# A fused attention and feed-forward kernel: all four-unit groups by 15 products per three feature blocks, and the scaling of r moved within the step for odd units

## The chip, the core and the metric

One core of one Trainium2 chip runs the whole kernel. The metric is the device time in microseconds (us) of one execution; the time of a kernel is the median of several runs.

## What is computed

Two blocks follow each other. The first is a linear attention with a decaying state; the second is a feed-forward block with a gate (SwiGLU), all in float32.

```python
for t in range(S):                     # r, k, v: (4, 8, 768, 48)
    cur = einsum(u * k[t], v[t])
    y[t] = einsum(r[t], state + cur)
    state = w * state + einsum(k[t], v[t])
x = y.transpose(0, 2, 1, 3).reshape(3072, 384)
g = x @ w_gate                         # (384, 1536)
out = (g * sigmoid(g) * (x @ w_val)) @ w_out     # w_out (1536, 384)
```

## The kernel before

**Units and groups.** The 3072 tokens are cut into 24 *units* of 128 tokens (`N`), in the order of time for all four batches at once. Attention turns unit i into a slice of `xT` (128 features x 3 x 128 tokens). Two units make a *group* g of 256 tokens for the feed-forward block, and from group 2 on the groups are worked in pairs g, g+1 (g even): such a pair, 512 tokens, is a *four-unit group*. The 1536 hidden features are 12 *feature blocks* f of 128.

**The feed-forward block.** Gate and value of a feature block are six 128x128 by 256-token matmuls per group if done directly. Groups 0 and 1 do that (`gate_value`, L451). The four-unit groups use forms with fewer products, in three kinds before the change:

- Groups 2 and 4: `four_units` (L648) with `four` (L599). Per feature block it makes 11 matmuls of 256 columns (L627), of sums of x (`x_sums`, L575: 4 VectorE additions per four-unit group) and sums of weights (`w_sums`, L585: 5 GpSimd additions of 128x256 per two feature blocks). Between the matmuls ScalarE copies partial results out of PSUM (L634), VectorE adds and multiplies (L637 to L645), ScalarE applies Silu (L607), and GpSimd makes one of the two products of gate and value (L611).
- Group 6: `three_beside` (L832) with `three_step` (L807). Per *three* feature blocks, called a round t of four, it makes 15 products, each of two matmuls of 256 columns (L817), one for the gate and one for the value. These are 120 matmuls per four-unit group. Each product is accumulated in one of the chains n, y, l4, l5, l1, l2, l8, each in a PSUM bank; ScalarE copies and VectorE additions of 128x512 (L842) take the chain's partial sums between the products, and the next product of a chain waits until its last sum is read. Silu is at L849. In rounds 0 to 2 GpSimd makes one gate-value product (z + 11.8) and VectorE two; value rows (`NR + 3 * j + i`) are written again in the next round.
- Groups 8 and 10: `three_units` (L927), the same products after the last unit, in the tail.

The 15-product forms need sums of x (`x_forms`, L761: 11 VectorE operations of 128x256), sums of weights (`w_forms`, L729: 9 GpSimd operations of 128x256 per round), and six of the weight blocks of every round replaced, once for good, by sums (`in_place`, L717: 6 GpSimd operations per round, 24 in all). `in_place` may run only after the last product with the plain weights. Before, 18 of the 24 run inside `four_units(4)` and the last 6 beside the projections that follow (`prepare_threes`, L791).

Each four-unit group ends in `two_projections` (L671): 14 products of 6 matmuls of 192 columns (L530), in the order of a list, with sums of the hidden values (`h_sums`, L495: 8 VectorE additions of 128x768) ahead of them. Tiles for sums of weights and for `h_sums` share one ring of three buffers (tag `w_bits`), so a new tile waits until the tile three before it is read. The first three pieces of the next group's products stand among the last four projections.

**Attention, by steps.** The loop over s (L1138) is written out by hand and sets the order on every engine. A step s from 12 on does in turn:

1. `own_sum(s)`; `scale(s+1)`: GpSimd scales k (L308) and r (L311) of unit s+1 from `k_ld`, `r_ld` into `hats`; `own_product(s+1)`: two more GpSimd operations (L235, L236); `load_v(s+1)` and `load(s+3)` on SyncE's queue.
2. `gaps(s, 0)`: pieces of the feed-forward work from `todo`. Then `scores(s-1)` (L382), `outputs(s-2)`, `update(s-2)`, and `gaps(s, 1)`.
3. `turn_blocks(s)` (L376): two VectorE transposes (L380) out of `blocks`. `move_blocks(s+1)` (L356): 16 small DMAs on SyncE's queue that bring `hats` of unit s+1 into `blocks`.
4. `gaps(s, 2)`, `diagonal(s)`, `gaps(s, 3)`, `gaps(s, 4)`.

From unit 12 on, units 2m and 2m+1 share one buffer for the scaled r (`rhat_of`, L110). So `scale_r` of an odd unit waits until the 16 DMAs of the even unit have read it. `gaps` hands out so many pieces per step that a four-unit group with its projections fills four steps; both `four_units` and `three_beside` give 26 pieces.

Of the kernel before, what the change touches and what calls it, by code (L numbers as in the profile page):

```python
# [9 lines left out]
FP32 = mybir.dt.float32  # L10
# [5 lines left out]
P = 128  # L16
# [6 lines left out]
def fast(  # L23
# [31 lines left out]
    N = B * NCH  # L55
# [29 lines left out]
    hTs = hv[:, 0:NR].rearrange("p (j f) t -> p j f t", j=2)  # L85
    sgs = cst.tile([P, 3, 2 * P], FP32, name="sgs")
    free_sg = deque(sgs[:, n] for n in range(3))
    free_part = deque(hv[:, NR + n] for n in range(6))

    banks = [ps_f.tile([P, 4 * P], FP32, name=f"bank{n}") for n in range(4)]  # L90
    free = deque(banks[:2])
# [1 line left out]
    def take():  # L93
        return free.popleft()
# [144 lines left out]
    def own_sum(i):  # L239
        dus[i] = three.tile([P, H], FP32, name="du", tag="du")  # L240
        dve.tensor_reduce(dus[i][:], rks.pop(i), axis=AX.X, op=ALU.add)
# [65 lines left out]
    def scale_k(i):  # L307
        pool.tensor_mul(khat[i % 4][:, :, 0:D], raw(i)[0], kscale)  # L308
# [11 lines left out]
    def scale(i):  # L320
        scale_k(i)
        scale_r(i)
# [187 lines left out]
    def project(g, n):  # L510
# [51 lines left out]

    PLACE = {
        "p1": 0, "p2": 3, "p6": 4, "c11": 5, "sg0": 6.5, "p7": 8, "p5": 9, "c22": 10, "p4": 12,
        "c21": 13, "p3": 17, "c12": 18, "sg1": 19.5, "h1": 24.5,
    }

    def x_halves(g):  # L570

        i = [2 * (g + j) % NX for j in range(2)]
        return [[xT[:, i[j] : i[j] + 2, c, :] for j in range(2)] for c in range(CC)]

    def x_sums(g):  # L575
        (x11, x12), (x21, x22), _ = x_halves(g)
        ta, tb = (two.tile([P, 2, 2, P], FP32, name=n, tag="w_low") for n in ("t12", "t34"))
        t1, t2, t3, t4 = ta[:, 0], ta[:, 1], tb[:, 0], tb[:, 1]
        dve.tensor_sub(t1, x12, x11)
        dve.tensor_sub(t2, x22, t1)  # L580
        dve.tensor_sub(t3, x22, x12)
        dve.tensor_sub(t4, x21, t2)
        part_of.setdefault(g, {})["t"] = (t1, t2, t3, t4)

    def w_sums(g, f):  # L585

        (w11, w12, w13), (w21, w22, w23) = (
            [w[:, c, P * f : P * (f + 2)] for c in range(CC)] for w in (wg, wv)
        )
        t = three.tile([P, 5, 2 * P], FP32, name="s", tag="w_bits")  # L590
        x = part_of.setdefault(g, {})
        x["s", f] = x["s", f + 1] = t
        pool.tensor_add(t[:, 0], w21, w22)
        pool.tensor_sub(t[:, 1], t[:, 0], w11)
        pool.tensor_sub(t[:, 2], w22, t[:, 1])
        pool.tensor_sub(t[:, 3], w12, t[:, 1])
        pool.tensor_sub(t[:, 4], w13, w23)

    def four(g, f, what):  # L599

        x = part_of[g]
        if what in ("p1", "p2"):
            x["ab"[what == "p2"], f] = take()
        h = [hT[g + j][:, f, :] for j in range(2)]
        if what in ("sg0", "sg1"):
            j = int(what[2])
            act.activation(h[j], h[j], AF.Silu)  # L607
            return
        if what == "h1":
            free_part.append(x.pop(("u3", f)))  # L610
            pool.tensor_mul(h[1], h[1], free_part[-1])  # L611
            return
        (w11, w12, w13), (_, w22, w23) = (
            [w[:, c, P * f : P * (f + 1)] for c in range(CC)] for w in (wg, wv)
        )
        (x11, _), (x21, x22), (x31, x32) = x_halves(g)
        s1, s2, s3, s4, s5 = (x["s", f][:, n, P * (f % 2) : P * (f % 2 + 1)] for n in range(5))
        t1, t2, t3, t4 = x["t"]
        acc, lhs, rhs, first = {
            "p1": ("a", w11, x11, True), "p6": ("a", s2, t2, False), "p7": ("a", s3, t3, False),  # L620
            "p4": ("a", w22, t4, False), "c21": ("a", w23, x31, False),
            "p2": ("b", w12, x21, True), "c11": ("b", w13, x31, False),
            "p5": ("b", s1, t1, True), "c22": ("b", w23, x32, False),
            "p3": ("b", s4, x22, False), "c12": ("b", s5, x32, False),
        }[what]
        ps = x[acc, f][:, 0 : 2 * P]
        pe.matmul(  # L627
            ps.rearrange("p (i t) -> p i t", i=2), lhs, rhs,
            start=first, stop=what not in ("p2", "p5", "p4", "p3"), skip_group_check=True,
        )  # L630
        if what in ("p1", "p6", "p7"):
            nm = {"p1": "p1", "p6": "u2", "p7": "u3"}[what]
            x[nm, f] = free_part.popleft()
            act.copy(x[nm, f], ps)  # L634
        elif what == "c11":
            free_part.appendleft(x.pop(("p1", f)))
            dve.tensor_add(h[0], free_part[0], ps)  # L637
        elif what == "c21":
            dve.tensor_mul(h[0], h[0], ps)
            free.append(x["a", f])  # L640
        elif what == "c22":
            dve.tensor_add(x["u3", f], x["u3", f], ps)
        elif what == "c12":
            free_part.appendleft(x.pop(("u2", f)))
            dve.tensor_add(h[1], free_part[0], ps)  # L645
            free.append(x["b", f])

    def four_units(g):  # L648

        steps = sorted((11 * f - 5 + at, f, what) for f in range(FC) for what, at in PLACE.items())  # L650
        if g + 2 == FIRST:
            steps += [
                (11 * f + 20 + 5.4 * m, f, do)
                for f in (2, 5, 8) for m, do in enumerate(in_place(f // 3))
            ]
            steps.sort(key=lambda x: x[0])
        pieces = [[] for _ in range(26)]
        n = 0
        for at, f, what in steps:
            if not isinstance(what, str):  # L660
                pieces[k].append(what)
                continue
            k = max(n - 1, 0) if n < 4 else 3 + min(23 * (n - 4) // (11 * FC - 4), 22)
            if what == "p1" and f % 2 == 0 and f + 2 < FC:
                pieces[k].append(lambda f=f: w_sums(g, f + 2))
            k = (0, 1, 2, 2)[n] if n < 4 else k
            pieces[k].append(lambda f=f, what=what: four(g, f, what))
            n += what[0] in "pc"
        return [lambda q=q: [do() for do in q] for q in pieces]

    def two_projections(g):  # L671

        def item(j, p):
            if g >= FIRST and (j, p) == (0, 1):
                for do in wide.pop("last"):
                    do()
            if (j, p) in ((1, 0), (0, 1)):
                h_sums(g, p)
            elif (j, p) in ((1, 1), (0, 3)):
                h_sums(g + 1, p // 3)  # L680
            elif g + 2 < FIRST:
                if (j, p) == (1, 2):
                    w_sums(g + 2, 0)
                elif (j, p) == (0, 6):
                    x_sums(g + 2)
            elif g + 2 < THREES and (j, p) == (0, 6):
                x_forms(g + 2)
            if FIRST <= g + 2 < N // 2:
                prepare_threes(g + 2, order.index(f"{j}{p}"))
            project(g + j, p)  # L690
        order = "00 10 01 02 11 04 03 12 05 06 13 14 15 16".split()
        return [lambda j=int(o[0]), p=int(o[1]): item(j, p) for o in order]


    FIRST, THREES = 6, 8
    ROUNDS = (
        ("r10", "n"), ("r14", "y"), ("r12", "l4"), ("r6", "l5"), ("r13", "n"), ("r2", "y"),
        ("r9", "l4"), ("r3", "l1"), ("r5", "n"), ("r11", "y"), ("r7", "l5"), ("r1", "l2"),
# [92 lines left out]
    def prepare_threes(g, n):  # L791
        if g >= THREES and n == 10:
            x_forms(g)
        if g > THREES:
            return
        if n == 1:
            if g == FIRST:
                todo_forms.extend(in_place(3))
            if g == THREES:
                todo_forms.extend(w_forms(g, 1))  # L800
        if n == 7:
            todo_forms.extendleft(reversed(w_forms(g, 0)))
        for _ in range(2):
            if todo_forms:
                todo_forms.popleft()()
# [26 lines left out]
    def three_beside(g):  # L832
# [19 lines left out]
        for t in range(4):  # L852
# [7 lines left out]
                ))  # L860
            if t < 3:
                forms = w_forms(g, t + 1)
                todo.append((z + 0.1, forms[0]))
                todo += [(z + n + 0.2, do) for n, do in enumerate(forms[1:])]
            gates = [[j * FC + 3 * t + i for i in range(3)] for j in range(2)]
            c = []
            for k in range(6):
# [146 lines left out]
    def queue(g):  # L1014
# [5 lines left out]
        elif g % 2 and g > 1:  # L1020
            first, *others = two_projections(g - 3)
            if g - 1 >= THREES:
                if g - 1 == THREES:
                    todo.extend((NW + 4, x) for x in others)
                return
            *pieces, last = (four_units if g - 1 < FIRST else three_beside)(g - 1)

            then = two_projections(g - 1)[0]

# [108 lines left out]
    for s in range(4, N + 2):  # L1138
        if 4 < s < N:
            own_sum(s)  # L1140
        if s + 1 < N:
            scale(s + 1)
            own_product(s + 1)
            load_v(s + 1)
            if s + 3 < N:
                load(s + 3)
        if s < BLOCKS:
            turn(s)
# [8 lines left out]
            gaps(s, 1)  # L1157
        if BLOCKS <= s < N:
            turn_blocks(s)
        if BLOCKS <= s + 1 < N:  # L1160
            move_blocks(s + 1)
        gaps(s, 2)
        if s - 2 >= 4 and (s < LATE or s > N):
            outputs(s - 2)
# [442 lines left out]
```

## Time and profile before

| what | value |
|---|---|
| median of 3 runs (lowest, highest) | 612.76 us (612.45, 613.14) |
| the profiled execution's own time | 612.62 us |
| its span, first to last instruction | 610.8 us |
| granted TensorE clock | 0.998 |
| busy: VectorE, ScalarE, GpSimd | 359.6, 233.0, 308.8 us |
| 15-product work of group 6, in the chain | from 341 to 412 us |
| 11-product work of groups 2 and 4, in the chain | 154 to 224 us, 252 to 318 us |

In the profile PE is TensorE's matmul and PEld its weight load, which overlap; DVE is VectorE, ACT ScalarE, POOL GpSimd, SP SyncE. A float32 matmul leaves two records. A group row gives line, engine, operation, output and inputs by tile name, shape and count, then busy us, mean ns of one, and the idle time of the engine just ahead of it with what ended it. A row of the chain of work that ended last gives start, duration, engine, tile, line and the number of records. In a timeline the brackets hold the idle time ahead of an instruction and its releaser.

### The profile page before, as it was taken

The page shows a single profiled execution, that of the slowest core. Times are in us where ns is not written, and L with a number is a line of the kernel's source. Part 1 is how long each engine was busy: PE and PEld are TensorE (multiplying, and loading weights), DVE is VectorE, ACT ScalarE, POOL GpSimd, SP SyncE. Part 2 cuts the span into 40 slices and gives each one's busy share as a digit, 9 for nine tenths or more (in the row PEclk, how much of TensorE's full clock was granted, in tenths as well). Part 3 has the DMA queues.
Part 4 walks back from the last instruction along what each step waited for, and adds up shares of the span by engine and source line. Part 5 has one row for each costly group of instructions (what it writes and reads, how often), then busy time and mean ns, then how long its engine had stood idle before and what let it go on. Part 6 is the DMA issues. An engine that isn't in the chain of part 4 may idle for free.

```text
span 610.8 us, 12619 instructions
## 1 busy us (share of the span) xinstructions
PE 595.3 (97%) x4968; PEld 537.3 (88%) x4968; DVE 359.6 (59%) x652; ACT 233.0 (38%) x574; POOL 308.8 (51%) x355
## 2 busy tenths in 40 slices
PE   8799999999999999999999999999999999999996
PEld 7588888899888899988899988889888889988896
DVE  6767876354444355335448368869537774477660
ACT  3368886321353522254431234442233430233310
POOL 4779888943829411867768766634425300001000
PEclk9999999999999999999999999999999999999999
DMA  7979882333332203222231412031000000100001
GB/s 168 237 206 247 236 293 56 68 59 66 74 51 44 44 14 74 65 44 43 52 48 27 87 40 42 13 51 29 27 28 1 0 1 14 39 1 1 2 1 56
DMA packets 138005, 40.44 MB, mean 66 GB/s; under 512 B 128592, under 2 KB 131792, under 8 KB 137936
## 3 DMA queue, kind: packets, MB, share of 16 engines
q1 hardware_dynamic: 134480, 34.82, 26.9%
q10 hardware_dynamic: 3456, 4.72, 2.2%
q8 instruction: 41, 0.67, 0.5%
q14 instruction: 28, 0.23, 0.1%
HBM read 28.51 MB, written 4.72 MB: 54 GB/s over the span
## 4 chain that ended last, share of the span: by engine, by line
PE 87%; POOL 2%; DVE 2%; ACT 1%; issue 1%; DMA 1%; SPq 0%; ACTq 0%; POOLq 0%
PE bank L530 26%; PE bank L627 19%; PE bank L817 13%; PE bank L456 7%; PE c_l L817 6%; PE y_ps L418 5%; PE c_n L817 3%; PE c_y L817 3%; PE s_ps L388 3%; POOL wgv L223 1%; PE u_ps L433 1%; PE tp L350 1%; DMA r_ld<-in_r_dram 1%; ACT At L329 0%; POOL hats L311 0%
## 5 line engine op out<-in xcount | busy, mean ns | idle before, releaser
L456 PE MATMUL bank<-xT,wgv 128*128 128x256 f32 x288 | 66.8, 385 | 0.6 <-ACT xT L422 0.6
L329 ACT ACTIVATE At<-ident,du 128x128 f32<-128x128 f32 x176 | 60.6, 397 | 15.7 <-DVE o_sb L543 7.2
L951 POOL TENSOR_TENSOR hv<-At,hats 128x512 f32<-128x512 f32 x8 | 10.2, 1273 | 107.1 <-ACT At L950 107.1
L627 PE MATMUL bank<-xT,wgv 128*128 128x256 f32 x240 | 64.3, 379 | 0.0
L456 PEld LDWEIGHTS bank<-xT,wgv 128*128 128x128 f32 x288 | 53.2, 190 | 8.9 <-ACT xT L422 0.8
L627 PEld LDWEIGHTS bank<-xT,wgv 128*128 128x128 f32 x240 | 45.4, 190 | 6.0
L530 PE MATMUL bank<-wo,hv 128*128 128x192 f32 x288 | 49.5, 327 | 0.0
L530 PEld LDWEIGHTS bank<-wo,hv 128*128 128x128 f32 x288 | 47.3, 190 | 0.5
L393 DVE COPY_PREDICATED At<-mask,s_ps 128x512 f32<-128x512 int32 x48 | 33.1, 743 | 22.2 <-PE s_ps L388 11.2
L634 ACT COPY hv<-bank 128x256 f32<-128x256 f32 x72 | 26.7, 371 | 46.5 <-PE bank L627 37.2
L530 PE MATMUL bank<-wo,hs 128*128 128x192 f32 x240 | 42.4, 326 | 1.2 <-DVE o_sb L546 1.2
L536 ACT COPY o_sb<-bank 128x192 f32<-128x192 f32 x36 | 11.3, 317 | 81.0 <-PE bank L530 77.4
L530 PE MATMUL bank<-wt,hs 128*128 128x192 f32 x240 | 41.9, 327 | 0.0
L530 PEld LDWEIGHTS bank<-wo,hs 128*128 128x128 f32 x240 | 39.7, 190 | 1.8 <-DVE o_sb L546 1.5
L627 PE MATMUL bank<-t,s 128*128 128x256 f32 x144 | 39.8, 383 | 0.0
L530 PEld LDWEIGHTS bank<-wt,hs 128*128 128x128 f32 x240 | 39.3, 190 | 0.5 <-issue 0.4
L311 POOL TENSOR_TENSOR hats<-r_ld,scales 128x384 f32<-128x384 f32 x20 | 20.0, 1002 | 38.5 <-DMA hats<-hats 38.5
L418 PE MATMUL y_ps<-At,v_ld 128*32 128x128 f32 x768 | 34.9, 273 | 1.3 <-DVE At L393 1.3
L842 DVE TENSOR_TENSOR hv<-hv,bank 128x512 f32<-128x512 f32 x44 | 29.3, 682 | 10.8 <-ACT hv L842 5.6
L817 PE MATMUL bank<-xf,wgv 128*128 128x256 f32 x128 | 33.0, 381 | 0.4 <-ACT o_sb L540 0.4
L418 PEld LDWEIGHTS y_ps<-At,v_ld 128*32 128x32 f32 x768 | 30.3, 110 | 2.4 <-issue 1.4
L418 PE MATMUL y_ps<-rT,Z 112*32 112x128 f32 x480 | 29.8, 276 | 0.6 <-ACT kT L354 0.6
(236 smaller groups left out, 1350.7 us busy)
## 6 DMA issues: line engine op xcount, KB each, us to landing
hats<-hats SPq DMA_DIRECT2D x192, 32.0 KB, 2.0
w_bits<-in_moe_w_gate_dram SPq DMA_DIRECT2D x6, 768.0 KB, 6.4
v_ld<-in_v_dram SPq DMA_DIRECT2D x48, 96.0 KB, 3.0
w_bits<-in_moe_w_val_dram SPq DMA_DIRECT2D x6, 768.0 KB, 6.1
w_bits<-in_moe_w_out_dram SPq DMA_DIRECT2D x6, 768.0 KB, 6.7
out_dram<-o_sb ACTq DMA_DIRECT2D x24, 192.0 KB, 1.9
k_ld<-in_k_dram SPq DMA_DIRECT2D x20, 192.0 KB, 3.0
r_ld<-in_r_dram SPq DMA_DIRECT2D x20, 192.0 KB, 3.9
```

Source lines behind the costliest of these rows:

```text
L311: pool.tensor_mul(rhat_of(i)[:, :, 0:D], raw(i)[1], rscale)
L329: lambda h=h: act.activation(At[i % 2][:, h, :], ident[:], AF.Identity, scale=du[:, h : h + 1])
L388: pe.matmul(ps[e][:, a, :], kT[i % 2][rows, at(i, a), :], turned[i][rows, at(i, a), :], start=True, stop=True, skip_group_check=True,)
L393: dve.copy_predicated(At[i % 2][:].rearrange("p (a e) t -> p a e t", e=2)[:, :, e], mask[:].bitcast(INT32).unsqueeze(1).to_broadcast([P, H ...
L418: pe.matmul(ps[32 * q : 32 * q + 32, cc, :], *x, start=start, stop=stop, skip_group_check=True,)
L456: pe.matmul(gv[:, o, :].rearrange("p (i t) -> p i t", i=2), wt[:, c, P * f : P * (f + 1)], xT[:, 2 * g % NX : 2 * g % NX + 2, c, :], start ...
L530: pe.matmul(ps, lhs[:, f, :], rhs[:, f, :], start=(f == 0 and n in (0, 1, 4)), stop=(f == FH - 1), skip_group_check=True,)
L536: act.copy({0: o1[:, 0:NH], 2: o1[:, NH:DM], 3: o2[:, NH:DM]}[n], ps)
L627: pe.matmul(ps.rearrange("p (i t) -> p i t", i=2), lhs, rhs, start=first, stop=what not in ("p2", "p5", "p4", "p3"), skip_group_check=True,)
L634: act.copy(x[nm, f], ps)
L817: pe.matmul(ps[:, o], u[:, o], v, start=first and o == 0, stop=True, skip_group_check=True,)
L842: do(out, *(pair_of(wide[a][:]) if isinstance(a, str) else a for a in args))
```

## The change

`FIRST`, the first group of the 15-product kind beside attention, goes from 6 to 2, and `four_units` with its helpers goes away. The order in which the sums of weights are made is spread anew. In even steps, for odd units from 13 on, `scale_r` and `load(s+3)` move down in the step. `scale_k` and `own_product` stay.

```diff
-    free_part = deque(hv[:, NR + n] for n in range(6))
...
-    PLACE = { ... }
-    def x_sums(g): ...
-    def w_sums(g, f): ...
-    def four(g, f, what): ...
-    def four_units(g): ...
...
     def two_projections(g):
...
-            elif g + 2 < FIRST:
-                if (j, p) == (1, 2):
-                    w_sums(g + 2, 0)
-                elif (j, p) == (0, 6):
-                    x_sums(g + 2)
             elif g + 2 < THREES and (j, p) == (0, 6):
                 x_forms(g + 2)
-            if FIRST <= g + 2 < N // 2:
+            if g + 2 < N // 2:
                 prepare_threes(g + 2, order.index(f"{j}{p}"))
...
-    FIRST, THREES = 6, 8
+    FIRST, THREES = 2, 8
...
             if g == FIRST:
-                todo_forms.extend(in_place(3))
+                todo_forms.extend(in_place(0) + in_place(1))
...
             if t < 3:
                 forms = w_forms(g, t + 1)
-                todo.append((z + 0.1, forms[0]))
-                todo += [(z + n + 0.2, do) for n, do in enumerate(forms[1:])]
+                if g == FIRST and t < 2:
+                    forms += in_place(t + 2)
+                start = z - 4 if t else 0
+                todo += [
+                    (start + (z + 10 - start) * n / len(forms) + 0.15, do)
+                    for n, do in enumerate(forms)
+                ]
...
-            *pieces, last = (four_units if g - 1 < FIRST else three_beside)(g - 1)
+            *pieces, last = three_beside(g - 1)
...
+        late = BLOCKS < s + 1 < N and s % 2 == 0
         if s + 1 < N:
-            scale(s + 1)
+            scale_k(s + 1)
+            if not late:
+                scale_r(s + 1)
             own_product(s + 1)
             load_v(s + 1)
-            if s + 3 < N:
+            if s + 3 < N and not late:
                 load(s + 3)
...
         if BLOCKS <= s < N:
             turn_blocks(s)
+        if late:
+            scale_r(s + 1)
         if BLOCKS <= s + 1 < N:
             move_blocks(s + 1)
+        if late and s + 3 < N:
+            load(s + 3)
         gaps(s, 2)
```

More of the change, by code (lines that the diff above doesn't have):

```diff
@@ L554, in project @@
             act.dma_start(out=out[n0 : n0 + P, :], in_=x["out"][j][:])
[L565 to L568, printed above, removed]
     def x_halves(g):
@@ L573, in x_halves @@
         return [[xT[:, i[j] : i[j] + 2, c, :] for j in range(2)] for c in range(CC)]
[L575 to L669, printed above, removed]
```

## The prediction

> **What bounds the kernel now.** I read the busy times first, then the stretches of the four-unit groups, PE's waits, the chain that ended last, and the timelines of GpSimd and VectorE. The page:
>
> ```profile
> PE 595.3 (97%) x4968; PEld 537.3 (88%) x4968; DVE 359.6 (59%) x652; ACT 233.0 (38%) x574; POOL 308.8 (51%) x355
> ```
>
> The stretches of group 2, group 4 and group 6 (start:end, length, then busy us of PE, PEld, DVE, ACT, POOL):
>
> ```profile
> 160.00:217.00 57.00, 57.00 (x374) 49.83 (x364) 24.56 (x56) 26.16 (x74) 30.92 (x42) 1.00 0.27 46
> 254.00:314.00 60.00, 60.00 (x457) 52.59 (x456) 26.69 (x60) 26.03 (x73) 42.36 (x59) 1.00 0.28 48
> 341.00:412.00 71.00, 69.97 (x570) 61.23 (x570) 46.44 (x74) 29.02 (x65) 44.61 (x57) 1.00 0.25 44
> ```
>
> PE has no idle time under group 2 and 4 (its waits from 124 to 341 us are an empty list). Under group 6, which already has the 15-product form, it has two:
>
> ```profile
> PE bank L817 <- DVE hv L842: 0.6, 1, 0.6
> PE bank L817 <- ACT o_sb L540: 0.4, 1, 0.4
> ```
>
> The chain (start, us, what, records) gives PE's real pace, which the 380 ns of a pipelined record hide:
>
> ```profile
> 182.94 33.87 PE bank L627 x156
> ...
> 360.44 4.53 PE bank L817 x20
> ...
> 369.90 17.75 PE bank L817 x80
> ```
>
> 33.87/156 = 217 ns for each record of 256 columns. A page speaks against taking this as the bound: the Trainium skill (Perfetto Trace Analysis, section Identifying the Most-Contended Engine) judges TensorE by its weight loads, not by matmul busy time. By that group 2's stretch is 49.83/57 = 87% full and a removed matmul is worth two loads of 190 ns, 48 x 0.19 = 9.1 us for what follows. The row decides: the records follow each other at 217 ns with nothing between, and at 19.50/120 = 162 ns for 192 columns, so the columns count.
>
> **Part 1, matmuls removed.** Groups 2 and 4 go from 12 x 11 = 132 to 4 x 15 x 2 = 120 matmuls each: 24 fewer, 48 records, 48 x 0.2165 = 10.4 us. All of it lies on PE, which is the chain there, and in the tail (446 to 577 us) PE is dense too: what is saved early is saved at the end, unless the new form makes PE wait.
>
> **Part 1, work exchanged on the others, per four-unit group.** VectorE: out go 48 operations of 0.42 and 4 of x, 22 us; in come 48 of 0.69 (33), 6 products of about 0.9 and 2 of 1.4 (8), 11 of x (4.9), 46 us. ScalarE: 36 x 0.371 + 24 x 0.416 = 23 out, 24 x 0.586 + 9 x 0.63 + 2 x 0.85 = 21 in. GpSimd: 30 x 0.727 + 12 x 0.744 = 31 out, 36 x 0.78 + 3 x 1.275 = 32 in. ScalarE and GpSimd stay equal in sum. VectorE: a round is 15 x 0.866 = 13 us of PE and 12 x 0.69 + 1.8 = 10.1 of VectorE; a step adds 1.39 + 0.74 + 1.37 + 0.55 = 4.0 of VectorE beside 3.1 of scores and outputs on PE. Below one, so no general bound, but with little slack where a round ends. The waits, priced by group 6:
>
> *a. The third bank.* r12 opens l4 with the bank that ScalarE's copy behind the fourth-last projection frees: 0.41 in group 6, built into the order: 2 x 0.4 = 0.8 (0 to 1).
>
> *b. The change of rounds.* From 360.44 to 387.65 PE's timeline has 120 records: 26.0 at pace, 27.2 taken, 1.2 lost at two changes: 0.8 where VectorE's transposes fell between the Silu products and the next chain's sum (the 0.6 above), 0.2 to 0.4 where not. By the pieces per step, group 4 has one such meeting (round 3, step 18) and two plain changes: 1.0. Group 2 has one near it (round 2, step 14): 0.8, a plain one 0.1, and a late GpSimd at the first change, below: 0.7. Sum 2.6 (0, if each falls beside the scores, to 6).
>
> *c. The end of the group.* The third projection needs two sums of hidden values. In group 6 the scores lie between (416.2 to 418.9) and hide a sum that ended at 417.75; in groups 2 and 4 they don't, and projections come straight after one another. Taking the reduction (0.54) and GpSimd's interference off, the sum would end near 416.6 where PE is ready at 416.2: 0.45 x 2 = 0.9 (0 to 2.4).
>
> **Part 1, GpSimd in group 2.** This is where all in-place sums now fall: 12 ahead of the group, beside the projections, 6 in each of its first two rounds.
>
> ```profile
> 123.76 1.00 POOL L308 TENSOR_TENSOR hats<-k_ld,scales 128x384 f32<-128x384 f32 x1
> 133.40 1.02 POOL L311 TENSOR_TENSOR hats<-r_ld,scales 128x384 f32<-128x384 f32 x1 [8.64 <-DMA hats<-hats]
> ...
> 147.41 0.73 POOL L593 TENSOR_TENSOR s<-wgv 128x256 f32<-128x256 f32 x1 [8.58 <-PE bank L530]
> ...
> 309.15 1.53 POOL L722 TENSOR_TENSOR wgv<-wgv 128x256 f32<-128x256 f32 x2
> ...
> 320.38 5.83 POOL L722 TENSOR_TENSOR wgv<-wgv 128x256 f32<-128x256 f32 x4
> ```
>
> An in-place sum takes 0.76 at 309 us and 1.46 at 320 us, where VectorE makes h sums (1.37 to 1.48 each there, 0.95 alone). The Trainium skill (GPSIMD Engine Reference, section Specifications) says that GpSimd's interfaces to SBUF are shared with VectorE and contended when VectorE has two SBUF inputs. By the rule all 12 beside the projections cost 1.46, 17.5 us; by the quiet row 9.2. Either fits: they have from 126.9 (both scalings of r out of the way) to 147.4, less 2.4 for the state's scaling at 136.4, because the first new sums wait for the projection that frees their ring buffer (the wait until 147.41). Cover of 3 to 4 us for VectorE's slower h sums: none is needed by PE within 2.5 us in the timeline, so nothing.
>
> From 147.4 GpSimd is full: 9 + 9 + 6 sums, three beside the x forms (2.6, as at 339.5), 21 at 0.745, 15.6; the scaling 3.85; the state 1.15. It reaches the first gate-value product at 170.7. PE starts round 1 at 160.25 + 12 x 0.866 = 170.6; ScalarE can take the new chain out only when that product (1.28) has read the value row, at 172.0 instead of about 171.7. So 0.3 to 0.5 late, in a place with some 0.2 slack (group 6: copies until 367.2, needed at 367.4). Round 2: 15 sums, 3 of scaling and 1.15 more put it at 187.9, against 187.3 needed: beside the transposes, so counted with them. This is the 0.7 of b, and its price is open: each 0.1 us on a sum costs 39 x 0.1 = 3.9 us.
>
> **Part 2, r of odd units.** Before, GpSimd sat 8.6, 11.7, 6.3 and 11.8 us at L311 (units 13, 15, 19, 23); PE did not wait, so nothing is gained by itself. What it buys is the 11.7 at 168 to 180 us, in which the new sums must run: without the move, b would be up to 11 us dearer. What is moved past: `own_product` and two gaps of sums on GpSimd go ahead of r, and behind r waits SyncE's queue: 16 DMAs (10.4 us to issue, 2.0 to land), the load of unit s+3 (0.37 + 0.57), then `load_v`. Before, the 16 began as the transposes ended (143.48 and 143.50). Now r can end 1 to 3 us after these (step 12, behind 12 in-place sums: about 146.5). The next transposes come at 165.6, with 6 us to spare; in the other even steps the next are 20 us and more away. At step 22, the shortest, r still waits for the same 16 DMAs until 407.4 and starts no later. The loads land 10 us or more ahead of use (the tightest, unit 23: issued at 380, landing 384, used 394.6). Cost 0 (0 to 1).
>
> **Sum.** 10.4 - (0.8 + 2.6 + 0.9) = 6.1 us. The profiled execution took 612.62 (610.8 of span, 1.8 around it): 606.5. The median is 0.14 above it: 606.7.
>
> **Rivals.** A measurement of this kernel can tell about 0.2%, 1.2 us, from no change.
> - *Waits nearly gone*: the sums of weights are spread more evenly and only the bank waits stay, 0.8 to 1.5: 603.5. For it: no wait at group 6's third change of rounds. Against: the order at the changes is group 6's. 16%.
> - *Waits eat most*: each of six changes costs 1.2, and the group ends 1.2: 10.4 - 0.8 - 6 - 2.4 = 1.2 to 3: about 610. VectorE's 46 us per group speak for it, the one named wait in group 6 against. 13%, and within 0.2% 5%.
> - *GpSimd becomes the bound of group 2*: at 0.93 us per sum in place of 0.745 the 39 sums on the way to the second change take 7.3 us more, and the kernel is slower by 1.2; at the 1.06 of sums beside VectorE's products (366 us) it is 619. Against: only x forms and Silu products have two SBUF inputs there. 6%.
> - *The forecast*, 604.5 to 609: 60%.
>
> The range 603.6 to 610.4 leaves out part of the first and of the last two. Faster 0.89, same 0.05, slower 0.06.
>
> **What would show it.** L627 gone, 480 records more at L817, PE's busy time near 585; PE waits of 0.4 at the third bank in both groups; PE waits on L842 with transposes just ahead; a short wait on L505 at each group's end; L311's waits gone for units 13, 15 and 19; at L749 a mean below 0.8. Wrong would be: PE waits on sums of weights (L749), on `kT` or `rT`, or more than 1.2 us lost at a change.

## The result and the profile after

| | before | after |
|---|---|---|
| median (lowest, highest) | 612.62 us (612.45, 613.14) | 608.24 us (607.97, 608.70) |
| ratio, 95% interval | | 0.9928 (0.9911 to 0.9945) |
| profiled execution, span | 612.62, 610.8 us | 608.25, 606.5 us |
| records on PE | 4968 | 4920 |

The change is faster by 4.4 us; 6.1 were forecast, and 608.24 lies within the range. Measured again beside other kernels, on another chip, the changed kernel took 607.71 us against 612.1, a ratio of 0.9939 (0.9925 to 0.9953). The page of the changed kernel:

```profile
PE 587.9 (97%) x4920; PEld 527.2 (87%) x4920; DVE 408.4 (67%) x682; ACT 228.2 (38%) x524; POOL 311.6 (51%) x349
```

The 48 records are gone, PE's busy time falls by 7.4 us and VectorE's rises by 49. The same three stretches as before, for groups 2, 4 and 6:

```profile
160.00:217.00 57.00, 56.84 (x505) 48.59 (x498) 45.14 (x68) 23.30 (x50) 41.56 (x53) 1.00 0.30 52
254.00:314.00 60.00, 58.43 (x449) 50.37 (x448) 45.14 (x67) 23.80 (x52) 35.46 (x42) 1.00 0.29 50
341.00:412.00 71.00, 69.69 (x571) 60.59 (x571) 50.94 (x78) 29.02 (x67) 45.35 (x55) 1.00 0.23 41
```

PE was full under groups 2 and 4; now 1.6 us are open under group 4 (60.00 against 58.43) and almost nothing under group 2. PE's waits from 124 to 430 us, a list that held only group 6's two before, name them (engine and tile, what it waited for, total us, times, longest):

```profile
PE bank L710 <- DVE hv L735: 2.0, 2, 1.3
PE bank L710 <- ACT o_sb L539: 1.1, 3, 0.4
PE bank L710 <- ACT hv L735: 0.3, 1, 0.3
```

One wait for VectorE of 1.3 us stands out. It is at 303.37, group 4's third change of rounds. VectorE's timeline there, then GpSimd's:

```profile
298.59 2.94 DVE L735 TENSOR_TENSOR hv<-hv 128x512 f32<-128x512 f32 x2 [0.78 <-ACT hv L742]
301.45 0.70 DVE L379 STREAM_TRANSPOSE kT<-hats 128x512 f32<-128x512 f32 x1
302.08 0.66 DVE L379 STREAM_TRANSPOSE rT<-hats 128x512 f32<-128x512 f32 x1
302.67 1.84 DVE L735 TENSOR_TENSOR hv<-hv,bank 128x512 f32<-128x512 f32 x3
```

```profile
296.66 1.00 POOL L310 TENSOR_TENSOR hats<-r_ld,scales 128x384 f32<-128x384 f32 x1
297.62 0.99 POOL L307 TENSOR_TENSOR hats<-k_ld,scales 128x384 f32<-128x384 f32 x1
298.58 1.00 POOL L310 TENSOR_TENSOR hats<-r_ld,scales 128x384 f32<-128x384 f32 x1
299.54 1.44 POOL L234 TENSOR_TENSOR rk<-r_ld,k_ld 128x384 f32<-128x384 f32 x1
301.06 1.33 POOL L235 TENSOR_TENSOR rk<-rk,scales 128x384 f32<-128x384 f32 x1
```

The two products of gate and value (both inputs in SBUF) take 2.94 us while GpSimd scales unit 20 and makes that unit's own product. The transposes stand behind them, and the first of the three sums at 302.67 frees the bank PE waits for. Stretch by stretch, from the starts in the chains of both profiles:

| part of the chain | before | after | lost against the matmuls removed |
|---|---|---|---|
| group 2's products | 149.21 to 224.23 | 149.32 to 220.75 | 5.2 - 3.59 = 1.6 |
| projections behind it, 120 records | 19.50 | 19.86 | 0.36 |
| group 4's products | 243.73 to 318.50 | 240.61 to 313.36 | 5.2 - 2.02 = 3.2 |
| projections behind it, 60 records | 9.75 | 10.02 | 0.27 |
| group 6's products | 341.31 to 412.28 | 336.44 to 407.92 | 0.51 |

10.4 less these 5.9 is 4.5; the start and the tail take 0.2, and the spans differ by 4.3.

### The profile page after: what moved, and what is told of

It reads as the page before. It is cut to its first block, busy times and chain, and to the rows that moved or that the text cites. A ratio compares the mean times of both kernels' runs of the same rounds, so it can differ in the third digit from the quotient of the medians.

```text
span 606.5 us, 12429 instructions
## 1 busy us (share of the span) xinstructions
PE 587.9 (97%) x4920; PEld 527.2 (87%) x4920; DVE 408.4 (67%) x682; ACT 228.2 (38%) x524; POOL 311.6 (51%) x349
## 4 chain that ended last, share of the span: by engine, by line
PE 83%; DVE 4%; POOL 3%; ACT 2%; issue 1%; DMA 1%; ACTq 0%; DVEq 0%; SPq 0%; POOLq 0%
PE bank L710 27%; PE bank L529 26%; PE bank L455 7%; PE c_l L710 6%; PE y_ps L417 5%; PE c_n L710 3%; PE c_y L710 3%; PE s_ps L387 3%; DVE hv L735 2%; POOL wgv L222 1%; PE u_ps L432 1%; PE tp L349 1%; DMA r_ld<-in_r_dram 1%; ACT hv L735 1%; ACT hv L742 1%
## 5 line engine op out<-in xcount | busy, mean ns | idle before, releaser
L735 DVE TENSOR_TENSOR hv<-hv,bank 128x512 f32<-128x512 f32 x132 | 87.5, 681 | 29.8 <-PE bank L710 16.8
L455 PE MATMUL bank<-xT,wgv 128*128 128x256 f32 x288 | 66.8, 385 | 0.6 <-ACT xT L421 0.6
L710 PE MATMUL bank<-xf,wgv 128*128 128x256 f32 x256 | 65.9, 382 | 1.1 <-ACT o_sb L539 1.1
L735 ACT COPY hv<-bank 128x512 f32<-128x512 f32 x72 | 40.3, 585 | 58.2 <-PE bank L710 43.4
L455 PEld LDWEIGHTS bank<-xT,wgv 128*128 128x128 f32 x288 | 53.2, 190 | 8.9 <-ACT xT L421 0.8
L710 PEld LDWEIGHTS bank<-xf,wgv 128*128 128x128 f32 x256 | 48.0, 190 | 8.6 <-ACT o_sb L539 1.8
L642 POOL TENSOR_TENSOR s<-wgv 128x256 f32<-128x256 f32 x39 | 29.3, 773 | 43.3 <-PE bank L529 43.3
L445 POOL TENSOR_TENSOR Z<-Z,w 48x192 f32<-48x192 f32 x32 | 17.3, 540 | 53.3 <-DVE Z L444 52.0
L710 PE MATMUL bank<-xT,s 128*128 128x256 f32 x152 | 36.4, 383 | 2.5 <-DVE hv L735 2.0
L742 ACT ACTIVATE hv<-hv 128x512 f32<-128x512 f32 (+1 forms) x33 | 21.2, 668 | 45.2 <-DVE hv L735 45.2
L710 PE MATMUL bank<-xT,wgv 128*128 128x256 f32 x144 | 35.9, 382 | 0.0
```

What stands on the lines that cost most here:

```text
L445: pool.tensor_mul(ze, ze, w)
L455: pe.matmul(gv[:, o, :].rearrange("p (i t) -> p i t", i=2), wt[:, c, P * f : P * (f + 1)], xT[:, 2 * g % NX : 2 * g % NX + 2, c, :], start ...
L642: op(made[o], made[a], made[b])
L710: pe.matmul(ps[:, o], u[:, o], v, start=first and o == 0, stop=True, skip_group_check=True,)
L735: do(out, *(pair_of(wide[a][:]) if isinstance(a, str) else a for a in args))
L742: todo.append((at, lambda: act.activation(gate, gate, AF.Silu)))
```

## The experiments

Theory A: group 4's excess loss is one serial chain on VectorE ahead of one matmul (products slowed by GpSimd, then transposes, then the sum), while the later r is what lets the sums of weights be ready at all. The rivals are in the expectations.

### Each part alone

The changed kernel with r always early:

```diff
-        late = BLOCKS < s + 1 < N and s % 2 == 0
+        late = False
```

> The changed kernel with part 2 undone: r of every odd unit is scaled at the start of its step again. Theory (part 1 needs part 2, since in group 2 GpSimd has no room for the wait for the 16 DMAs): GpSimd stands some 10 us at L310 for unit 15 in the middle of group 2, its sums of weights come late, PE waits for them there, and the kernel takes 4 to 10 us more than the changed one, 612 to 618. Rival (part 2 is idle bookkeeping, as in the kernel before where no PE wait followed GpSimd's): within 1 us of the changed kernel.

616.97 us (613.64 to 618.66), ratio 1.0080 (1.0067 to 1.0093): slower than before the change. GpSimd's timeline of this kernel in step 12:

```profile
132.98 1.01 POOL L310 TENSOR_TENSOR hats<-r_ld,scales 128x384 f32<-128x384 f32 x1 [8.72 <-DMA hats<-hats]
...
135.99 7.23 POOL L615 TENSOR_TENSOR wgv<-wgv 128x256 f32<-128x256 f32 x6
...
149.67 2.63 POOL L642 TENSOR_TENSOR s<-wgv 128x256 f32<-128x256 f32 x3
```

It stands 8.72 us ahead of unit 13's r, so the 12 in-place sums begin at 136, and the first sums of weights at 149.67 instead of 147.45. Unit 15's r, at which the expectation placed the wait, then stands nowhere (179.82, straight after k). PE waits five times, 4.6 us in all, for ScalarE's copies, which wait for GpSimd's gate-value product: 2.07 us in group 2, and 2.52 in group 4, where unit 19's r had stood 5.90. The profiled execution took 613.64 us, the shortest of the six.

The kernel before with the later r alone (of the diff, the hunks on `late` and nothing else):

```diff
+        late = BLOCKS < s + 1 < N and s % 2 == 0
...
-            scale(s + 1)
+            scale_k(s + 1)
+            if not late:
+                scale_r(s + 1)
...
+        if late:
+            scale_r(s + 1)
```

> The kernel before with part 2 alone: r of odd units scaled later, groups 2 and 4 still by 11 products. Theory (part 2 has no gain or loss of its own): within 0.5 us of the kernel before, and GpSimd's waits at the scaling of r shrink. Rival (the later r makes the block moves late): slower by 1 us or more, with PE waiting for the transposed blocks.

612.88 us (612.48 to 614.19), ratio 1.0013 (1.0004 to 1.0022). Group 6's products take 71.75 us in the chain (340.37 to 412.12) instead of 70.97. So part 2 gains nothing by itself and costs 0.8 us where the 15-product form already was.

### The serial chain of group 4

Transposes of units 18 and 20 ahead of the sums of their step:

```diff
         if 4 <= s - 1 < N:
...
+            if s in (18, 20):
+                turn_blocks(s)
             gaps(s, 1)
-        if BLOCKS <= s < N:
+        if BLOCKS <= s < N and s not in (18, 20):
             turn_blocks(s)
```

> The changed kernel with the two VectorE transposes of units 18 and 20 put ahead of the middle gap of their steps, so that they no longer stand between the Silu products and the sums of the next round (group 4's last change of rounds and group 6's first). Theory A (everything that stands on VectorE between the products and the next sum makes PE wait, transposes and slowed products alike, one after the other): PE's wait of 1.3 us near 302 us goes or shrinks to 0.2 to 0.5, that of 0.6 near 365 us goes, the kernel is 1.5 to 2 us faster than the changed one. Theory B (only the products slowed by GpSimd count, the transposes fit beside them): less than 0.5 us.

606.21 us (605.79 to 606.62), ratio 0.9899 (0.9885 to 0.9914), on a chip where the kernel before took 612.03 us and the changed one has no time (as for the next kernel). Both waits for VectorE, 1.3 and 0.6 us, are gone. The products are still slow, but the sums follow them at once:

```profile
298.51 2.70 DVE L735 TENSOR_TENSOR hv<-hv 128x512 f32<-128x512 f32 x2 [0.87 <-ACT hv L742]
301.13 1.87 DVE L735 TENSOR_TENSOR hv<-hv,bank 128x512 f32<-128x512 f32 x3
```

Unit 20's r and its products with k made in step 18 instead of 19, so that GpSimd is quiet beside VectorE's products:

```diff
-            if not late:
+            if not late and s != 19:
                 scale_r(s + 1)
-            own_product(s + 1)
+            if s != 19:
+                own_product(s + 1)
+            if s == 18:
+                scale_r(20)
+                own_product(20)
```

> The changed kernel with the scaling of r and the own product of unit 20 made one step earlier on GpSimd, so that GpSimd is quiet when VectorE makes the Silu products at group 4's last change of rounds. The computation is the same. Theory A: there the two products take 1.3 to 1.9 us in place of 2.9, PE's wait near 302 us shrinks by about 1 us, and the kernel gains about that, 607.2, if the three operations added a step earlier cost nothing there. Rival (the transposes alone make that wait): products quicker, PE's wait unchanged, no gain. If GpSimd's gate-value product one round earlier comes late for it, a loss shows at that change of rounds instead.

606.06 us (605.75 to 607.04), ratio 0.9900 (0.9886 to 0.9915). The transposes are where they were; the pair of products has shrunk from 2.94 to 1.29, and PE's wait of 1.3 us is gone (group 6's 0.6 stays):

```profile
297.99 1.29 DVE L735 TENSOR_TENSOR hv<-hv 128x512 f32<-128x512 f32 x2 [0.78 <-ACT hv L742]
299.20 0.70 DVE L379 STREAM_TRANSPOSE kT<-hats 128x512 f32<-128x512 f32 x1
299.83 0.67 DVE L379 STREAM_TRANSPOSE rT<-hats 128x512 f32<-128x512 f32 x1
300.43 1.84 DVE L735 TENSOR_TENSOR hv<-hv,bank 128x512 f32<-128x512 f32 x3
```

The changed kernel again, beside the runs of the next part:

> The changed kernel itself beside the other kernels of this call, on their chip. Every theory: 0.9928 of the kernel before (608.2 us where that is 612.6).

607.71 us (607.52 to 609.4), as told above. Both edits in one kernel:

> The changed kernel with both edits of the two runs before: transposes of units 18 and 20 ahead of the sums of the step, and unit 20's r scaled and its product with the keys made at the start of step 18. Theory A (transposes and slowed products are two terms of one serial chain ahead of one matmul): the first edit left a wait of 0 there, so the second can add nothing at that change; what is left is unit 20's transposes in group 6, 0.3 to 0.6: 0.989 of the kernel before. Rival (two independent losses): 2.0 and 2.2 add up to 4.2, 0.986.

605.49 us (605.48 to 605.55), ratio 0.9893 (0.9877 to 0.9908), 2.2 us below the changed kernel beside it, not 4.2. The stretch from 28 records of round 2 to the projection behind the third change says it by itself: 26.26 us in the changed kernel (283.42 to 309.68) and 26.28 when it was run again; 25.23 with the transposes early, 24.62 with unit 20 early, 24.82 with both. The two are terms of one sum: either edit takes the 1.3 us wait away, and gives back 1.0 or 1.6 of the 2.1 us lost there. PE's last record ends at 600.59 us in the second trace of the changed kernel, and 1.5, 1.6 and 2.3 us earlier in these three; what both have over unit 20 alone is group 6's wait of 0.6.

### Where the later r is needed

The new form for group 4 alone, r early throughout (the kernel before with one number changed):

```diff
-    FIRST, THREES = 6, 8
+    FIRST, THREES = 4, 8
```

> The kernel before with the 15-product form taken for group 4 (and 6) only; group 2 keeps four units by blocks, r of all units stays early, and the sums of weights keep group 6's spacing. Removed: 12 matmuls, 24 records, 5.2 us. Lost: bank 0.4, end of the group 0.3. Theory A (group 4's 2.1 us at its third change comes from the scaling of units 19 and 20 that the later r pushes onto VectorE's products): with r early these meet elsewhere, the changes lose about 1, so a saving of 3.5 (ratio 0.9943). Rival B (the changes of a group with two transposes lose about 2.5 whatever the place of r): saving 2.0 (0.9967). Rival C (r early makes GpSimd wait for unit 19's load and the changes then wait for GpSimd): saving below 1 or a loss (0.9985 or more).

616.27 us (615.33 to 616.77), ratio 1.0067 (1.0053 to 1.0081): rival C, and theory A's number is far off. 5.2 us of matmuls are gone, and the kernel is slower by 4.2. In the trace PE's last record ends 1.2 us later than before (606.76 against 605.55 us); another 2.2 us of the longer span lie behind it, and what made them is not shown. GpSimd, then PE:

```profile
293.81 1.02 POOL L311 TENSOR_TENSOR hats<-r_ld,scales 128x384 f32<-128x384 f32 x1 [6.58 <-DMA hats<-hats]
...
302.47 1.26 POOL L842 TENSOR_TENSOR hv<-hv 128x512 f32<-128x512 f32 x1
```

```profile
304.40 3.60 PE L817 MATMUL bank<-xf,s 128*128 128x256 f32 x8 [2.94 <-ACT hv L842]
```

Unit 19's r waits 6.58 us; six sums of weights queue behind it, then the gate-value product, 7.0 us later than in the changed kernel (295.43), while group 4 began only 2.4 later (242.98 against 240.61); ScalarE's copy waits for that and PE for the copy. And the eight records after the wait take 3.60 us where 1.99 is usual. The stretches of 1 us there (the third number from the end is the granted TensorE clock):

```profile
304.00:305.00 1.00, 0.60 (x2) 0.57 (x3) 0.09 (x1) 1.00 (x3) 1.00 (x2) 0.88 0.00 0
305.00:306.00 1.00, 1.00 (x4) 0.43 (x3) 1.00 (x1) 0.87 (x2) 1.00 (x2) 0.50 0.00 0
...
307.00:308.00 1.00, 1.00 (x4) 0.81 (x3) 1.00 (x2) 0.00 (x0) 0.92 (x2) 0.50 0.00 0
308.00:309.00 1.00, 1.00 (x4) 0.51 (x3) 1.00 (x3) 0.00 (x0) 0.45 (x1) 0.92 0.00 0
```

This wait costs twice: once as a wait, and again at half clock after it.

The changed kernel with the later r for unit 13 alone:

```diff
-        late = BLOCKS < s + 1 < N and s % 2 == 0
+        late = s == 12
```

> The changed kernel with the later r for unit 13 alone (step 12); units 15, 17, 19, 21 and 23 as before the change. Theory A (part 2's worth is GpSimd's wait for unit 13's load ahead of the 12 in-place sums, and later it only pushes scaling onto the changes of rounds): group 6 gets its 0.5 us back and group 4's third change 1 to 2: 606 us, 0.990. Rival (unit 19's wait for its load, 6.3 us before, holds the sums and the gate-value product of group 4 up as unit 13's did in group 2): 1 to 3 us slower than the changed kernel, 0.995 to 0.998. Equal to the changed kernel (0.9928) if the two cancel or neither counts.

615.72 us (614.97 to 616.41), ratio 1.0064 (1.0050 to 1.0078), 8.0 us above the changed kernel beside it: more than the rival named. Unit 15's r stands 3.23 us and PE then 3.56 (193.81); unit 19's stands 5.32 and PE 1.56 and 0.39 behind it. Group 4's third change waits 1.33 us, as in the changed kernel, so the later r did not make that wait. Units 15 and 19 need the move as well. The later r for units 13, 15 and 19, with both cures:

```diff
-        late = BLOCKS < s + 1 < N and s % 2 == 0
+        late = s in (12, 14, 18)
```

> Both cures, with the later r for units 13, 15 and 19 alone; units 17, 21 and 23 early as before the change. Theory A (the later r is needed where GpSimd has new sums to make and only in the way elsewhere): group 6's 0.3 to 0.5 us come back, 605.0, 0.9885. Rival (unit 17's or 23's wait, 11.8 us before for 23, now holds something up): at or above both cures alone, 0.9893 or more.

605.35 us (605.22 to 606.44), ratio 0.9888 (0.9871 to 0.9904). Group 6's products take 57.62 us from 343.55 to 401.17, and 58.11 with both cures alone, so 0.5 comes back there: the pair of products at group 6's third change takes 1.28 us again, and 2.00 with both cures alone. In the total it can't be told from both cures alone (0.9893).

### Two edits in group 2

Unit 16's r in step 14 too, with both cures: it lies beside the products of group 2's third change, which take 2.88 us in the changed kernel.

```diff
-            if not late and s != 19:
+            if not late and s not in (15, 19):
...
-            if s == 18:
-                scale_r(20)
-                own_product(20)
+            if s in (14, 18):
+                scale_r(s + 2)
+                own_product(s + 2)
```

> Both cures (transposes of units 18 and 20 early, unit 20's r scaled two steps early), and unit 16's r as well (in step 14), which lies beside VectorE's two products at group 2's third change (2.89 us there, 1.29 when GpSimd is quiet). Theory A (a slowed pair of products delays the sum that frees PE's bank): up to 0.8 us of group 2's loss comes back, 0.988 of the kernel before, the pair takes 1.3. Rival (no PE wait is named there, so the pair is hidden, and two scalings more in step 14, where GpSimd is full, delay its gate-value product of the second change by 4 us): 2 to 4 us slower than both cures alone, 0.993 to 0.996.

608.89 us (607.87 to 609.76), ratio 0.9946 (0.9930 to 0.9962): the rival, 3 us slower than both cures alone. VectorE's pair is quick now, and the third change 0.5 us shorter (24.32 us from 194.34 to 218.66, 24.82 from 192.05 to 216.87 in the changed kernel); but GpSimd comes to its second gate-value product at 190.89 instead of 188.58. VectorE, then PE:

```profile
206.21 1.29 DVE L735 TENSOR_TENSOR hv<-hv 128x512 f32<-128x512 f32 x2 [0.78 <-ACT hv L742]
```

```profile
192.82 1.13 PE L710 MATMUL bank<-xf,s 128*128 128x256 f32 x4 [2.33 <-ACT hv L735]
```

The same with the later r for units 13, 15 and 19 alone:

> The last two edits with both cures: unit 16's r in step 14, later r for units 13, 15 and 19 alone. If each edit gains by itself the two add, 0.987; if unit 16 costs in group 2, that cost less 0.5 us.

608.06 us (607.45 to 609.47), ratio 0.9933 (0.9917 to 0.9950): the cost of unit 16's edit, again.

The sums of weights where they stood before the change, one per product from the start of the round:

```diff
-                start = z - 4 if t else 0
-                todo += [
-                    (start + (z + 10 - start) * n / len(forms) + 0.15, do)
-                    for n, do in enumerate(forms)
-                ]
+                todo.append((z + 0.1, forms[0]))
+                todo += [(z + n + 0.2, do) for n, do in enumerate(forms[1:])]
```

> The changed kernel with the sums of weights placed as before the change (one per pair of records from the start of the round) in place of the even spread that starts four places earlier; in group 2 the six in-place sums then come last of a round. Theory A (GpSimd is the limit in group 2 and each change waits for its gate-value product): sums start later, group 2's changes wait 1 us or more, 0.995. Rival (the order among GpSimd's own operations counts little, since it works without a pause): 0.993, as the changed kernel.

608.23 us (608.05 to 609.31), ratio 0.9930 (0.9914 to 0.9945): no difference from the changed kernel, so the spread has no share in the result that these runs can tell. GpSimd's gate-value products come at 171.44 and 188.63, as in the changed kernel (171.38, 188.58), because three in-place sums slip behind each of them.

## Why the prediction was nearly right

| term | forecast | measured in the profile |
|---|---|---|
| matmuls removed | 10.4 | 10.4 (48 records) |
| a, third bank | 0.8 | 0.29 + 0.41 = 0.7 |
| b, changes of rounds, group 2 | 1.6 | 1.6 - 0.29 = 1.3 |
| b, changes of rounds, group 4 | 1.0 | 3.2 - 0.41 = 2.8 |
| c, end of the group | 0.9 | 0.36 + 0.27 = 0.63 |
| part 2 | 0 | 0.5, in group 6 |

**The mis-sized term is b of group 4.** The forecast had "one such meeting (round 3, step 18) and two plain changes: 1.0". Meeting and place were right: transposes between products and sum, in that round. Its size was group 6's, 0.8, and it was 2.1: from 292.84 to 309.68 PE's chain has 68 records, 14.7 us at pace, in 16.84. What was sized wrong is the pair of products ahead of the transposes. The forecast priced them at about 0.9 each, as in group 6, where GpSimd makes sums of weights beside them:

```profile
366.19 1.86 DVE L842 TENSOR_TENSOR hv<-hv 128x512 f32<-128x512 f32 x2 [0.78 <-ACT hv L849]
```

Beside the scaling of a unit the pair takes 2.94 us, and this 1.08 is most of the 1.3 that the forecast lacks at this meeting. Beside a quiet GpSimd the pair takes 1.29, and the run with unit 20 early shows that difference, 1.65, come back as 1.64 of PE's stretch. The rule that the forecast cited (the Trainium skill, GPSIMD Engine Reference, section Specifications: interfaces shared with VectorE, contended when VectorE has two SBUF inputs) was right here; it was weighed for GpSimd's sums, and not for VectorE's own products, on which PE waits. The transposes stayed at 0.70 beside the same scaling, and sums with one input in PSUM at 0.69 beside GpSimd's sums of weights (group 4 alone, 296 to 300 us). The two plain changes lost 0.16 and 0.5 (GpSimd's product at 279.67).

**Luck.** The terms a, b of group 2 and c came out 0.7 below their forecast together, which hid part of the 2.3 that b of group 4 and part 2 went over. Within group 2 the forecast put 0.7 on the first change of rounds, 0.8 on the second and 0.1 on the third. PE's chain leaves room for 0.36 around the first (80 records in 17.68 us) and 0.16 around the second (44 in 9.69), and the third loses some 0.5 to VectorE's pair of products, by the run with unit 16's r early.

**Part 2 was "cost 0".** It costs 0.5 here and 0.8 alone, both in group 6. The forecast counted what would be late, and not what would come early. At group 6's third change, before and after:

```profile
396.77 1.28 DVE L842 TENSOR_TENSOR hv<-hv 128x512 f32<-128x512 f32 x2
...
394.59 1.01 POOL L308 TENSOR_TENSOR hats<-k_ld,scales 128x384 f32<-128x384 f32 x1
```

```profile
391.90 2.01 DVE L735 TENSOR_TENSOR hv<-hv 128x512 f32<-128x512 f32 x2
...
390.68 1.00 POOL L234 TENSOR_TENSOR rk<-r_ld,k_ld 128x384 f32<-128x384 f32 x1
391.76 1.00 POOL L235 TENSOR_TENSOR rk<-rk,scales 128x384 f32<-128x384 f32 x1
```

Before, GpSimd stood 11.8 us at unit 23's r behind the scaling of k, and so was quiet beside VectorE's pair. With r moved, unit 23's own product no longer stands behind that wait and runs beside the pair; the 40 records there take 9.34 us instead of 8.83. Part 2 alone has the same 9.34, and 0.27 more at the first change, where unit 21's r falls beside the pair. The queues it was moved past, where the forecast looked for a price, cost nothing visible: no wait of PE on `kT`, `rT` or a load appeared in these stretches.

**What part 2 buys.** "Up to 11 us dearer" without it: 616.97 against 608.24 is 9 us in the medians; in the traces PE's last record ends 5.3 us later (606.44 against 601.18), and the other executions have no trace. The forecast listed the waits of units 13, 15, 19 and 23, and counted only unit 15's. The runs show that unit 13's (8.72 us ahead of the in-place sums), unit 15's (3.23, PE 3.56) and unit 19's (6.58, PE 2.94) each reach PE. "PE did not wait, so nothing is gained by itself" was right for the 11-product form, as the run with part 2 alone shows.

**GpSimd in group 2.** In-place sums beside the projections, forecast between 0.76 and 1.46 each, took 1.07 to 1.09; the first two gate-value products were forecast at 170.7 and 187.9 and came at 171.38 and 188.58. (The terms named for the second add up to 187.2.) The price per sum, by which the third rival stood or fell, stayed below its 0.93: the 39 sums from 147.4 to 188.6 us took 29.0 us, 0.744 each, against the forecast's 0.745. Over the whole kernel the means (in ns, behind the busy time) are below the 0.8 named as a sign:

```profile
L642 POOL TENSOR_TENSOR s<-s 128x256 f32<-128x256 f32 x39 | 30.5, 782 | 0.9
L642 POOL TENSOR_TENSOR s<-s,wgv 128x256 f32<-128x256 f32 x39 | 29.5, 757 | 2.8
L642 POOL TENSOR_TENSOR s<-wgv 128x256 f32<-128x256 f32 x39 | 29.3, 773 | 43.3 <-PE bank L529 43.3
```

But the slack is small, as that rival held: three operations more in step 14 put a wait of 2.33 us on PE.

**The other signs.** L627 is gone; the banks' waits came at 0.4 and below; GpSimd's waits at the scaling of r fell from four (38.5 us) to one (9.4 us). PE's busy time is 587.9 instead of near 585: of the 5.9 us lost only 2.4 are named as waits (3.4 from 124 to 430 us, 1.0 before), and the rest stands in rows that count as busy. No short wait on the sums of hidden values is named at a group's end; c shows only as projections that take 0.3 us longer, and its cause is not settled. "More than 1.2 us lost at a change", named as a sign of error, did come: the 2.1 above. The rival "waits eat most" has a slip: six changes at 1.2 us are 7.2, not 6, which leaves 0 in place of its 1.2.

## What to carry to other kernels

When work is exchanged between engines, price each operation on the chain at the speed that it has beside its new neighbours, not at its mean: the same pair of products took 1.29 or 2.94 us. Terms that stand in one queue ahead of one wait are cured once, so two cures are not worth their sum; moving either the cause of the slowness or the transposes gave 1.5 to 2 us, and both gave 2.2. A wait on an engine off the critical path can shield another engine: GpSimd's wait for unit 23's r kept VectorE's pair at 1.28 us. And a move that gains nothing by itself (part 2 alone, 1.0013) can be what another change lives on: without it 0.9928 turns into 1.0080.

The quickest versions were both cures with the later r for three units (605.35 us, 0.9888) and both cures alone (605.49 us, 0.9893), against 0.9928 to 0.9939 for the change.

## What was not expected of the hardware

A pause of TensorE can cost again after it has ended. After PE waits of 2.13 us (r always early), 2.94 (group 4 alone) and 3.56 (unit 13 alone) the granted clock fell to 0.50 for about 3.4 us, some 1.7 us of work each time (an estimate, half of 3.4); after one of 2.33 (unit 16 early) and the 1.33 of the changed kernel the profile shows 1.00. The Trainium skill (TensorE: Matmul & The Clock Gate, section What's actually happening) gives half clock after an idle window of about 3.4 us that runs free of the program; the half and its length agree, but here two of the three pauses, 2.13 and 2.94 us, were shorter than that window. What decides between 2.13, which was enough, and 2.33, which was not, stays open. The three kernels' other executions show mean clocks of 0.990 to 0.995, where the changed kernel has 0.997 and more; that they hold more such stretches is likely, but only one execution of each has a trace.
